# Six more tiles of a second matmul by seven products instead of eight, three tiles ahead of a batch's first

## The chip, the cores and the metric

The kernel runs on one core of one Trainium2 chip. The metric is the time of one execution on the device, in microseconds (us). The engines are TensorE (PE; its weight loads are shown as PEld), VectorE (DVE), ScalarE (ACT), GpSimd (POOL) and SyncE (SP); they run side by side and wait for each other by semaphores. Matmuls write PSUM; VectorE and ScalarE read PSUM and write SBUF; DMA engines move data between SBUF and DRAM, or within SBUF.

## The reference

Two layers follow each other. The first takes x of 8 batches, 3008 positions and 256 channels (float32), transforms it along the positions (a real FFT), mixes the channels of the real and imaginary parts by a complex 256x256 matrix with a bias, shrinks each part towards zero by 0.01, and transforms back:

```
X = np.fft.rfft(x, axis=1)
Yr = Xr @ w_r - Xi @ w_i + b_r
Yi = Xr @ w_i + Xi @ w_r + b_i
Y  = soft_shrink(Yr, 0.01) + 1j * soft_shrink(Yi, 0.01)
y  = np.fft.irfft(Y, n=3008, axis=1)
```

The second takes the 24064 rows of y as tokens:

```
h = y @ w_in                 # 256 -> 2048
g = s * relu(h)**2 + b       # s and b are single numbers
out = g @ w_out              # 2048 -> 256
```

## The kernel before

**Transforms.** 3008 = 94 x 32, so each Fourier transform is two short ones, done as matmuls (helpers `s1_units`, `s23_units`, `s4_units`), with two trips through DRAM for each batch (ud and us, vd and vs). Each unit is one or a few matmuls into a PSUM bank of the pool psf (two banks) and one cast out of it, by VectorE or ScalarE: u (96x512), xf, v (128x512), yt (128x470). The shrinking is a chain of VectorE operations on the tile ring (lines 714 to 716; for the last two pairs of frequencies it is followed by eight copies, line 727). Batch b+1 is transformed while the second layer works on batches before it.

**Second layer.** The tokens are cut into 48 tiles in a fixed order (`_tile_order`): 12 wide ones of batches 0 and 1, then for each of the batches 2 to 7 five main tiles of 512 tokens, and some tail tiles (512 or 384 tokens from the ends of two batches) behind or between them. `mark[b]` is the place of the first tile of batch b, in steps of 1/16 tile: tiles 12, 17, 23, 29, 35 and 41 for batches 2 to 7.

The main loop goes through the tiles, 16 steps each. Step mc of tile ti does three things: planned units of the transforms; the first matmul of 128 hidden rows (`first_mm`, two matmuls of 512 columns into psh, two buffers of two banks); and a sixteenth of the second matmul of the tile before, ti - 1. So a tile's own stretch of time holds its first layer, and its products follow in the next stretch. At every odd step ScalarE takes the ReLU of two banks (line 871, tile rt), and then the square is written to gt in float16, by VectorE (line 884) or ScalarE (line 881). Which engine does a square or a cast is fixed when the program is built: `act_first` compares the estimated loads that `work` has added up. A scheduler then sets the order on each engine.

**Two ways to do the second matmul.** `second_mms` is the plain one: 4 blocks of 128 tokens by 16 blocks of hidden rows, 64 matmuls of 256 columns, and two operations of VectorE (line 945, 128x512) that scale by s, add the bias and write ost. `seven_mms` is a scheme of Strassen and Winograd: hidden rows and tokens are halved, and seven products of sums of quarters replace eight, 112 matmuls of 128 columns. The sums of quarters of the squares (`s_op`, line 980, 128x1024 in float16) are numbered 1 to 4 and made once for each half q of the hidden rows:

```
1: s1  = a21 + a22        3: a21 = a11 - a21
2: a11 = a11 - s1         4: a12 = a12 + a11   (an accumulating DMA from GpSimd's queue, line 973)
```

Sums 1 and 3 of q=0 are put at steps 10 and 11 of the tile's own stretch, the others at steps 2 to 5 of the next. Sums of the right-hand side (T_s) are made once. The products lie in two psa banks that are used in turn: products 1 and 2 share a bank, then product 3, then 4 and 5, then 6 and 7. `leave` takes them out by VectorE: eight operations of line 1012 (ost or zz from psa; seven of 128x256 and one of 128x512) and one of line 1030. Group 0 of `leave` (zz, then ost, then line 1030) empties the bank of products 1 and 2, which product 4 needs at the end of step 6. The seventh product, which reads the result of sum 4, begins at step 13.

`seven(ti)` says which tiles go that way: all full ones from the first tile of batch 7 on save the last two, tiles 4 to 6, and the two tiles ahead of each batch's first tile, as far as they have 480 or 512 tokens: 17 tiles.

**Queues.** GpSimd's queue issues the loads of x (line 234), the accumulating DMAs, and a copy into the tail tile (line 805), in the order that the scheduler gave. SyncE's queue issues the trips through DRAM, 32 KB moves within ring, and the stores.

Of the kernel before, what the change touches and what calls it, by code (L numbers as in the profile page):

```python
# [11 lines left out]
ALU = mybir.AluOpType  # L12
# [84 lines left out]
def kernel(  # L97
# [14 lines left out]
    B, S, D = x.shape  # L112
# [4 lines left out]
    MC = DFF // P  # L117
# [59 lines left out]
    def work(engine, us):  # L177
        load[engine] = max(load[engine], pe["now"]) + us
# [636 lines left out]
    def sub_size(tl):  # L815
        return 4 * tl[3] if tl[0] == "wide" else P
# [13 lines left out]
    def halves(ti):  # L830
        return width(tiles[ti]) in (480, 512)
# [129 lines left out]
    def part(ti, q, i, k):  # L961
        size = 2 * sub_size(tiles[ti])
        return gts[(ti, q)][:, i, k, :, 0:size]

    def s_op(ti, n, q):

        size = 2 * sub_size(tiles[ti])
        if n == 1:
            sums[(ti, q)] = spool.tile([P, 4, 2 * P], F16, name="s1", tag="s1")
        s1 = sums[(ti, q)][:, :, 0:size]  # L970
        a11, a12, a21, a22 = (part(ti, q, i, k) for i in range(2) for k in range(2))
        if n == 4:
            nc.gpsimd.dma_start(out=a12, in_=a11, accum_op=ALU.add)  # L973
            return
        out, a, b, op = {
            1: (s1, a21, a22, ALU.add),
            3: (a21, a11, a21, ALU.subtract),
            2: (a11, a11, s1, ALU.subtract),
        }[n]
        nc.vector.tensor_tensor(out=out, in0=a, in1=b, op=op)  # L980
        work("dve", 0.07 + size / 480.0)

    def seven_mms(ti):
# [76 lines left out]
        for at, n, q in ((2, 2, 0), (2, 1, 1), (2, 4, 0), (3, 3, 1), (4, 2, 1), (5, 4, 1)):  # L1060
            at += alone and at > 3
            slots[at].append(lambda n=n, q=q: s_op(ti, n, q))
# [4 lines left out]
    def seven(ti):  # L1067
        if ti >= len(tiles) - 2 or not halves(ti):
            return False
        firsts = [mark[b] // MC for b in range(2, B)]  # L1070
        return (
            ti >= firsts[-1] or 4 <= ti < 7 or any(m - 2 <= ti < m for m in firsts)
        )

    plan = {}
# [18 lines left out]
    mark = {}  # L1094
# [32 lines left out]
    for ti in range(ti_n + 1):  # L1127
        nxt = [[]] * MC
        if ti:
            nxt = seven_mms(ti - 1) if seven(ti - 1) else second_mms(ti - 1)  # L1130
        for mc in range(MC):
            if ti < ti_n:
                for u in plan.pop(ti * MC + mc, []):
                    u()
                first_mm(ti, mc)
                if mc in (10, 11) and seven(ti):
                    s_op(ti, 1 if mc == 10 else 3, 0)
            for u in nxt[mc]:
                u()
# [31 lines left out]
```

## Time and profile before

| | |
|---|---|
| median of 3 runs | 840.88 us (838.2 to 841.81) |
| the profiled execution | 838.19 us, span 836.4 us |
| granted TensorE clock | 1.00 |
| squares on VectorE, line 884 | 254, of 128x1024 mean 1223 ns |
| squares on ScalarE, line 881 | 130, of 128x1024 mean 1060 ns |
| ReLU on ScalarE, line 871 | 384, of 128x1024 mean 1027 ns |
| sums of quarters, line 980 | 102, 128x1024 some 687 ns |
| products out, line 1012 | 136, 128x256 some 479 ns, 128x512 some 748 ns |
| plain sums out, line 945 | 59, 128x512 some 748 ns |
| sum 4, line 973 | 34, 857 ns on GpSimd, 4.7 us from issue to landing |

How to read it: busy time is the time that an engine has an instruction in it, as a share of the span of 836.4 us; instructions overlap a little at their ends, so the distance from start to start is less than the duration. A matmul's end is modelled, so a busy TensorE is not one at its peak, and here too the distance from start to start counts. The stretches by tile that follow begin at the first psh matmul of a tile.

### The profile page before, as it was taken

Reading aid. Unit: us, or ns where it says so; the run is one execution under the profiler, and the core shown is the slowest. Engines: PE = TensorE matmul, PEld = TensorE weight load, DVE = VectorE, ACT = ScalarE, POOL = GpSimd, SP = SyncE. Lnnn points to the kernel's source line nnn. Section 1 sums busy time; section 2 is a strip of 40 time slices with the busy share of each in tenths; the row PEclk is TensorE's granted clock in tenths of the full one; section 3 lists DMA queues with packets and bytes.
Section 4 is the critical chain, followed back from the end, with each engine's and each line's share of the span. In section 5 each row is a group of like instructions: output and inputs, shape, how many; then the busy total and the mean of one; then the engine's idle time right before and its main releaser. Section 6 shows DMA issues by size and latency. Waiting matters only on the chain.

```text
span 836.4 us, 19090 instructions
## 1 busy us (share of the span) xinstructions
PE 824.2 (99%) x7470; PEld 598.7 (72%) x7470; DVE 698.8 (84%) x1061; ACT 712.2 (85%) x953; POOL 79.8 (10%) x106
## 2 busy tenths in 40 slices
PE   8999999999999999999999999999999999999997
PEld 7857767777677767777677776777767777767765
DVE  5988989978898888877888788787889878889885
ACT  5998988998899989988899888988879888788882
POOL 4550001100011001100010000100001000001000
PEclk9999999999999999999999999999999999999999
DMA  8954578345873378534772258713565133513321
GB/s 201 183 150 103 120 181 213 64 96 132 199 185 65 98 181 198 126 88 116 192 190 65 81 131 206 180 47 97 127 177 138 48 97 90 140 45 76 72 66 61
DMA packets 115516, 105.04 MB, mean 126 GB/s; under 512 B 12646, under 2 KB 100714, under 8 KB 114082
## 3 DMA queue, kind: packets, MB, share of 16 engines
q1 hardware_dynamic: 102498, 80.55, 34.0%
q0 software_dynamic: 12928, 23.27, 17.6%
q8 instruction: 58, 0.95, 0.5%
q14 instruction: 32, 0.26, 0.1%
HBM read 53.52 MB, written 46.66 MB: 120 GB/s over the span
## 4 chain that ended last, share of the span: by engine, by line
PE 81%; DVE 8%; ACT 5%; DMA 3%; issue 2%; POOL 0%; SPq 0%; DVEq 0%; ACTq 0%; POOLq 0%
PE psh L175 33%; PE psa L175 30%; PE psf L175 17%; ACT rt L871 2%; DVE gt L884 2%; DVE gt L980 1%; DMA ring<-ring 1%; DMA x<-in_x_dram 1%; PE psm L175 1%; ACT gt L881 1%; DVE s L980 1%; DVE ost L1012 1%; ACT u L187 1%; DMA vd<-v 0%; DVE zz L1012 0%
## 5 line engine op out<-in xcount | busy, mean ns | idle before, releaser
L871 ACT ACTIVATE rt<-psh 128x1024 f32<-128x1024 f32 (+2 forms) x384 | 387.0, 1009 | 67.4 <-PE psh L175 65.2
L175 PEld LDWEIGHTS <-gt 128*128 128x128 f16 (+1 forms) x3568 | 303.7, 101 | 171.1 <-DVE gt L884 0.5
L175 PE MATMUL psh<-yt,w_in 128*128 128x512 f16 (+1 forms) x1344 | 396.5, 378 | 0.1
L884 DVE TENSOR_TENSOR gt<-rt 128x1024 f16<-128x1024 f32 (+2 forms) x254 | 304.9, 1204 | 88.6 <-ACT rt L871 86.8
L175 PE MATMUL psa<-w_out_t,gt 128*128 128x256 f16 (+3 forms) x2512 | 333.1, 258 | 0.0
L175 PEld LDWEIGHTS <-w_in 128*128 128x128 f16 x1536 | 137.3, 98 | 25.9 <-issue 3.2
L881 ACT ACTIVATE gt<-rt 128x1024 f16<-128x1024 f32 (+2 forms) x130 | 134.8, 1037 | 3.2
L187 ACT CAST u<-psf 96x512 f16<-96x512 f32 x96 | 55.7, 581 | 9.3 <-PE psf L175 8.6
L175 PE MATMUL psa<-T_s,gt 128*128 128x128 f16 (+1 forms) x752 | 63.5, 219 | 0.0
L699 DVE TENSOR_TENSOR ring<-psf,s 128x512 f16<-128x512 f32 x84 | 57.6, 685 | 4.2 <-PE psf L175 3.1
L187 ACT CAST v<-psf 128x512 f16<-128x512 f32 x82 | 47.5, 582 | 14.2 <-PE psf L175 13.3
L973 POOL DMA_DIRECT2D gt<-gt x34 | 31.1, 916 | 262.3 <-PE psh L175 86.3
L234 POOL DMA_DIRECT2D x<-in_x_dram x36 | 19.3, 540 | 386.3 <-PE psf L175 337.7
L175 PEld LDWEIGHTS <-xf 128*128 128x128 f16 x504 | 47.4, 98 | 7.2 <-DVE xf L672 1.7
L175 PE MATMUL psh<-tail,w_in 128*128 128x512 f16 (+1 forms) x192 | 52.1, 352 | 0.0
L175 PE MATMUL psf<-W_g,xf 128*128 128x256 f16 x336 | 50.4, 272 | 0.0
L945 DVE SCALAR_TENSOR_TENSOR ost<-psa,s_bc,bias_bc 128x512 f32<-128x512 f32 (+2 forms) x59 | 43.0, 730 | 4.5 <-PE psa L175 2.3
L187 ACT CAST yt<-psf 128x470 f16<-128x470 f32 (+2 forms) x84 | 43.2, 534 | 3.4 <-PE psf L175 2.2
L187 ACT CAST xf<-psf 128x512 f16<-128x512 f32 x67 | 39.1, 584 | 4.3 <-PE psf L175 4.1
L175 PE MATMUL psf<-x,A_t 94*96 94x512 f16 x102 | 38.9, 382 | 1.7 <-ACT yt L187 0.3
L175 PE MATMUL psf<-C_t,vs 96*128 96x94 f16 (+1 forms) x484 | 37.9, 205 | 0.0
L1012 DVE SCALAR_TENSOR_TENSOR ost<-psa,s_bc,zz 128x256 f32<-128x256 f32 (+1 forms) x64 | 28.8, 479 | 5.4 <-PE psa L175 3.6
(118 smaller groups left out, 758.2 us busy)
## 6 DMA issues: line engine op xcount, KB each, us to landing
out_dram<-ost SPq DMA_DIRECT2D x152, 128.0 KB
ud<-u SPq DMA_DIRECT2D x56, 192.0 KB
us<-ud SPq DMA_DIRECT2D x28, 384.0 KB
vd<-v SPq DMA_DIRECT2D x42, 256.0 KB
vs<-vd SPq DMA_DIRECT2D x14, 768.0 KB
x<-in_x_dram POOLq DMA_DIRECT2D x28, 376.0 KB, 6.5
ring<-ring SPq DMA_DIRECT2D x280, 32.0 KB
gt<-gt POOLq DMA_DIRECT2D x30, 256.0 KB, 4.6
```

The lines of the kernel that those rows point to most:

```text
L175: return nc.tensor.matmul(out, lhs, rhs, **how)
L187: return None, nc.scalar.copy(out=dst, in_=src)
L234: nc.gpsimd.dma_start(out=t[0:N1, i * w : (i + 1) * w], in_=xv[:, c * XCH * D + i * w : c * XCH * D + (i + 1) * w],)
L699: nc.vector.tensor_tensor(out=ring[0][:, i % 4], in0=ps, in1=hold[i // 2][:, i % 2].unsqueeze(1).to_broadcast([P, 2, D]), op=ALU.add,)
L871: nc.scalar.activation(out=rt[:, :, 0:w], in_=ps[:, :, 0:w], func=AF.Relu)
L881: nc.scalar.activation(out=gt, in_=rr, func=AF.Square)
L884: last_square[0] = nc.vector.tensor_tensor(out=gt, in0=rr, in1=rr, op=ALU.mult)
L945: nc.vector.scalar_tensor_tensor(out=ost[0:size, 0:k], in0=ps[0:size, 0:k], scalar=s_bc[0:size], in1=bias_bc[0:size].unsqueeze(1).to_broad ...
L973: nc.gpsimd.dma_start(out=a12, in_=a11, accum_op=ALU.add)
L980: nc.vector.tensor_tensor(out=out, in0=a, in1=b, op=op)
L1012: nc.vector.scalar_tensor_tensor(out=out, in0=of, scalar=s_bc[0:size], in1=other, op0=ALU.mult, op1=ALU.add)
```

## The change

`seven` takes three tiles ahead of a batch's first in place of two. That adds tiles 9, 14, 20, 26, 32 and 38: the fourth tile of batch 1 (in its order of six), the third of batch 2, and the fourth of batches 3, 4, 5 and 6. For these six the fourth sum of q=1 is an addition on VectorE (float16, 128x1024); that of q=0 stays a DMA. Everything else follows from the planner and the scheduler.

```diff
+    def third_last(ti):
+        return any(ti == mark[b] // MC - 3 for b in range(2, B))
+
     def s_op(ti, n, q):
...
-        if n == 4:
+        if n == 4 and not (q == 1 and third_last(ti)):
             nc.gpsimd.dma_start(out=a12, in_=a11, accum_op=ALU.add)
             return
         out, a, b, op = {
             1: (s1, a21, a22, ALU.add),
             3: (a21, a11, a21, ALU.subtract),
             2: (a11, a11, s1, ALU.subtract),
+            4: (a12, a12, a11, ALU.add),
         }[n]
...
         firsts = [mark[b] // MC for b in range(2, B)]
         return (
-            ti >= firsts[-1] or 4 <= ti < 7 or any(m - 2 <= ti < m for m in firsts)
+            ti >= firsts[-1] or 4 <= ti < 7 or any(m - 3 <= ti < m for m in firsts)
         )
```

## The prediction

> **What bounds the kernel now.** I read the busy table first, then the chain that ended last, then busy time by tile, then VectorE in order of time.
>
> ```profile
> PE 824.2 (99%) x7470; PEld 598.7 (72%) x7470; DVE 698.8 (84%) x1061; ACT 712.2 (85%) x953; POOL 79.8 (10%) x106
> PE 81%; DVE 8%; ACT 5%; DMA 3%; issue 2%; POOL 0%; SPq 0%; DVEq 0%; ACTq 0%; POOLq 0%
> ```
>
> TensorE is busy 99% of the span and carries 81% of the chain: a shorter matmul stream shortens the kernel, if nothing else becomes late. VectorE and ScalarE have some 15% left on average. An average hides the stages, so here are five stretches, each exactly the sixteen steps of one tile: the fourth and fifth tile of batch 3, the tail tile behind them, and two tiles at the end of the program with no transform work beside them.
>
> ```profile
> 388.28:405.90 17.62, 17.62 (x127) 12.19 (x125) 15.62 (x25) 15.33 (x22) 0.54 (x1) 1.00 0.56 140
> 405.90:421.33 15.43, 15.43 (x107) 10.32 (x106) 12.46 (x13) 11.80 (x17) 0.93 (x2) 1.00 0.84 211
> 421.33:437.41 16.08, 16.05 (x211) 12.05 (x209) 14.42 (x22) 15.32 (x22) 1.88 (x3) 1.00 0.82 201
> 735.61:747.76 12.15, 12.15 (x84) 7.84 (x81) 9.00 (x12) 9.87 (x11) 0.21 (x1) 1.00 0.15 45
> 747.76:760.92 13.16, 13.16 (x146) 9.38 (x144) 12.88 (x18) 10.68 (x11) 1.70 (x2) 1.00 0.34 71
> ```
>
> Columns: stretch, length, then busy time of PE, weight loads, VectorE, ScalarE, POOL, then granted clock (1.00 throughout), DMA. In the third stretch a seven-product tile leaves its sums: VectorE and ScalarE are busy 14.42 and 15.32 of 16.08. In the second, where the change puts another such tile, they are busy 12.46 and 11.80 of 15.43. That is free time in sum, but the question is when it comes. VectorE in the third stretch, in order of time (start, duration):
>
> ```profile
> 421.53 0.75 DVE L945 SCALAR_TENSOR_TENSOR ost<-psa,s_bc,bias_bc 128x512 f32<-128x512 f32 x1
> 422.20 1.22 DVE L884 TENSOR_TENSOR gt<-rt 128x1024 f16<-128x1024 f32 x1
> 423.34 0.69 DVE L980 TENSOR_TENSOR gt<-gt,s 128x1024 f16<-128x1024 f16 x1
> 423.94 0.69 DVE L980 TENSOR_TENSOR s<-gt 128x1024 f16<-128x1024 f16 x1
> 424.54 1.22 DVE L884 TENSOR_TENSOR gt<-rt 128x1024 f16<-128x1024 f32 x1
> 425.68 0.68 DVE L980 TENSOR_TENSOR gt<-gt 128x1024 f16<-128x1024 f16 x1
> 426.28 0.64 DVE L189 CAST yt<-psf 128x470 f16<-128x470 f32 x1
> 426.84 0.68 DVE L980 TENSOR_TENSOR gt<-gt,s 128x1024 f16<-128x1024 f16 x1
> 427.44 0.48 DVE L1012 SCALAR_TENSOR_TENSOR zz<-psa,s_bc,bias_bc 128x256 f32<-128x256 f32 x1
> 427.95 0.48 DVE L1012 SCALAR_TENSOR_TENSOR ost<-psa,s_bc,zz 128x256 f32<-128x256 f32 x1
> ```
>
> and TensorE at the end of it:
>
> ```profile
> 427.97 0.50 PE L175 MATMUL psa<-T_s,gt 128*128 128x128 f16 x6
> 428.49 0.23 PE L175 MATMUL psa<-T_s,s 128*128 128x128 f16 x1
> ```
>
> VectorE runs without a gap from 421.53 to 428.43. The fourth product (psa<-T_s,s) needs the PSUM bank that the last row frees; six small matmuls take 0.34 us in free running (0.056 each), so TensorE was ready at 428.31 and began at 428.49: a stall of 0.2 us. This hand-over limits such a tile. From the start of L945 to the restart of TensorE it is 6.96 us.
>
> **The change, part by part.** One step is the start-to-start distance in gapless rows, smaller than the printed duration: square 1.14 (422.20 to 423.34), sum 0.60, psf cast 0.56 to 0.60, L945 0.67, L1012 0.40, or 0.51 where it reads its predecessor's output.
>
> *TensorE.* The stretch at 735.61 has 32 matmuls of 512 columns and 48 of 256, the one at 747.76 has 32 of 512 and 112 of 128. A pair of 512 steps 0.43 in the timeline, 6.88 for 32. That leaves 5.27/48 = 0.110 per 256 and 6.28/112 = 0.056 per 128 columns. A tile: 64 x 0.110 = 7.03 before, 112 x 0.056 = 6.28 after, 0.74 us less without rounding. Six tiles: -4.4 us, the whole possible gain, 0.5% of the span. The weight loads, 112 for 64, hide: in the last stretch 144 of them are busy 9.38 of 13.16.
>
> The Trainium skill, "TensorE: Matmul & The Clock Gate", section "Back-to-back issue gap", speaks against this step: in a stream of weight load and matmul pairs it gives about 81 ns per matmul at 128 columns. By that a tile would cost 9.1 us instead of 6.28. The trace disagrees: 0.056.
>
> *VectorE and ScalarE.* Each new tile adds six sums (first two in its own stretch, four in the next), a seventh for the second half of the fourth sum, eight L1012 and one L1030 in place of two L945. The planner answers: 29 squares go from VectorE to ScalarE (254 to 225, 130 to 159), and 15 evacuations of psf the other way (v 82 to 75, yt 84 to 78, u 96 to 94 on ScalarE). In sum VectorE gets 42 x 0.60 + 42 x 0.40 + 6 x 0.67 + 6 x 0.33 - 12 x 0.67 - 29 x 1.14 + 15 x 0.58 = some 15 us, ScalarE 29 x 0.96 - 15 x 0.48 = some 20 us, over six groups of three tiles. The idle time of the three stretches above covers that in sum; its place is what costs.
>
> *The bank in the new tile's stretch* (second row above). In the changed order VectorE has, from L945 to the freeing row, the same ten instructions, except that the yt cast is gone and the new fourth sum stands between the two L1012: -0.56 - 0.51 + 0.40 + 0.60, so 6.89 us instead of 6.96. L945 starts at 406.13 before. In the stretch ahead VectorE runs gapless from 395.3 to 408, and gets two sums (+1.20) and a cast of v (+0.60), loses a square (-1.14), and the sums fill 0.25 of waits in the chain L714 to L716: +0.41, so 406.54, and the bank is free at 413.43. TensorE reaches the fourth product one matmul ahead of the psh pair that starts at 412.85, less 7 x 0.046 for seven shortened steps: 412.48. Stall 0.95. Four of the six new tiles (the fourth of batches 1, 3, 4 and 5) have this order: 4 x (0.95 - 0.74) = +0.8. Bounds: 0.2 (the row above) to 1.5 (VectorE later by another half square). The new sum itself waits for the third sum and for the second product's reading, both over by then; behind it on VectorE stands the row that frees the bank, and TensorE waits for that.
>
> *The third tile of batch 2* (its stretch begins at 282.9, that of its products at 302.4). A cast of v moves to VectorE behind the ring copies, which end at 301.95 before and, by +1.05 of sums and a square taken out behind them, at 302.9 after. TensorE wants that bank at 302.23 and gets it at 303.64: 1.4, while a stall of 0.4 on a v cast by ScalarE behind it goes. Then a second v cast and both squares stay in front: bank free at 312.25, TensorE there at 311.0: 1.25. Together 1.4 - 0.4 + 0.1 + 1.25 - 0.74 = +1.6. Bounds -0.3 and +2.4.
>
> *The fourth tile of batch 6*: no transform of a next batch beside it. VectorE begins 0.05 later, the order is the same; bank free 713.4, TensorE there at 712.8: 0.6 - 0.74 = -0.15.
>
> *The tile behind.* It starts with three L1012 instead of one L945 (+0.53). In the two groups with a 512-wide tail behind (421.3, 622.8) a square stays on VectorE that waits for its ReLU, and ScalarE now squares first: that ReLU moves from 425.08 to 425.6, the bank from 428.4 to 429.3 against TensorE at 428.3: +0.85 each, +1.7; bounds 0 and 1.9. In the other four a square leaves VectorE: -0.2 in the two before a 384-wide tail, 0 and +0.1 in the others, -0.3 in sum.
>
> *POOL and SP.* One accumulating DMA per new tile (0.86 us on POOL, landing in 4.7), behind one load of x and ahead of the next. It waits for the second sum, about as late as that load's own wait before (409.62), and the load is used over a tile later; the result is read by the seventh product, ten steps (9 us) after. If that cover went, the seventh product would wait 1 to 3 us (landings differ by up to 4.6, from 3.2 to 7.8). The stores are as many as before. Nothing for these.
>
> **The sum** (each term holds its share of the -4.4): 0.8 + 1.6 - 0.15 + 1.7 - 0.3 = +3.7; for waits on psf banks behind the moved casts, 0 to 0.3 in a group, I take 0.05, since their next user is a step away: +4.0. Against the profiled execution (838.19, 1.8 more than its span of 836.4) that is 842.2. The median of the runs, 840.88, is 2.7 above it, so I forecast 844.9.
>
> **The rivals.** *The gain survives.* If VectorE is not late at the hand-over, each stall is the 0.2 of the third stretch: 6 x (0.2 - 0.74) = -3.2; with none -4.4, so 836.5 to 837.7. For it: at 421.3 to 437.4 both engines are 90 and 95% busy and TensorE stands 0.2 us. Against it: there L945 starts as soon as its matmuls end, 0.2 us into the stretch, here at 0.64, and TensorE comes 0.5 sooner. It decides below a stall of 0.74.
>
> *The lag does not drain.* ScalarE gets 20 us more; if its ReLUs fall behind in the tiles before and after the batch's first, psh stalls too: another 1 us in each group, +10, 851. Against it: 1.3 us of idle time on VectorE at 429.7 in the tile behind.
>
> *Weight loads bind.* If each small matmul had to wait for its own load, 98 to 101 ns by the rows of the loads, a tile would take 112 x 0.098 = 11.0 for 7.0: 6 x 4 = +24, 865. The stretch at 747.76 is against it: 144 loads and matmuls without a stall. By the 81 ns of the page named above it would be 6 x 2.1 = +12, 853.
>
> *The DMA is late*: 6 x 1 to 3 on top, 851 to 863.
>
> **How the numbers follow.** Stalls as worked out 66%, the gain survives 15%, no drain 13%, DMA late 5%, weight loads 1%. The likeliest case's own bounds are +0.5 and +8: 841 to 849. The range takes in half of the first rival and most of the second: 838.5 to 851. About 0.5% (4.2 us) is what a measurement of this kernel can tell from no change. Slower by more: a little over half of the first case and the last three, 55%. Faster by more: half of the rival, 8%. Between: 37%.
>
> **What would show it.** Waits of PE psa for ost of VectorE, 1.4 us in four places now, become 8 to 10 us in ten or more; the stretch of each new product stays at 15.4 to 15.8 instead of 14.7; a wait of psf<-ring,T_t for a cast of v appears near 302. I am wrong if those stretches are 14.7 to 15.0, or if the added time stands in waits for psh or for DMA.

## The result and the profile after

The changed kernel takes 845.5 us (median of 6 runs, 842.81 to 847.25), the kernel before 839.25 in the same series (837.85 to 841.81). The ratio is 1.0068, 95% interval 1.0051 to 1.0085: slower by more than the 0.5% that can be told from no change. The profiled execution took 844.8 us, its span is 843.0. The forecast was 844.9 us, and "slower by more than that" with a chance of 0.55.

The busy table and the chain of the kernel after:

```profile
PE 822.4 (98%) x7758; PEld 600.1 (71%) x7758; DVE 713.2 (85%) x1131; ACT 732.2 (87%) x967; POOL 84.4 (10%) x112
...
PE 73%; DVE 11%; ACT 6%; DMA 6%; issue 2%; POOL 0%; SPq 0%; DVEq 0%; ACTq 0%; POOLq 0%
```

TensorE has less to do, and its share of the chain falls from 81 to 73%. VectorE, ScalarE and DMA take the rest: TensorE now waits for them in places where it did not.

What TensorE waited for from 195 to 840 us (the sum, how often, the longest), first in the kernel after, then in the kernel before, where a second row (0.3 for a cast of v) is left out:

```profile
PE psa L175 <- DVE ost L1016: 7.6, 10, 1.0
PE psf L175 <- DMA ud<-u: 0.7, 1, 0.7
PE psf L175 <- DMA vs<-vd: 0.5, 1, 0.5
```

```profile
PE psa L175 <- DVE ost L1012: 0.6, 2, 0.3
```

The ten places of the first row are the hand-over of the product bank in all six new tiles and in four of the tiles behind them. Over the whole span the wait for that bank goes from 1.4 us in four places to 8.4 us in twelve; two of them, in tiles 5 and 7, lie ahead of this window and are the same in both kernels (0.23 and 0.58).

Three stretches by tile, the same as before: the tile ahead, the stretch of a new tile's products, the tile behind (length, then busy PE, weight loads, VectorE, ScalarE, POOL, granted clock, DMA):

```profile
390.96:408.58 17.62, 17.62 (x126) 12.19 (x124) 15.70 (x27) 15.50 (x22) 0.54 (x1) 1.00 0.56 143
408.58:424.49 15.91, 14.87 (x154) 10.25 (x153) 14.38 (x20) 14.22 (x19) 1.81 (x3) 1.00 0.86 199
424.49:441.37 16.88, 16.05 (x211) 12.11 (x209) 15.03 (x23) 15.95 (x24) 2.16 (x4) 1.00 0.87 209
```

The middle stretch shows both halves of the story. PE is busy 14.87 of 15.91 us; before it was 15.43 of 15.43. The saving of TensorE is there, and a stall that is larger stands beside it. VectorE and ScalarE have free time left in this stretch (14.38 and 14.22 of 15.91), so it is not their sum that is short. VectorE in order of time shows where the stall comes from:

```profile
409.30 0.74 DVE L945 SCALAR_TENSOR_TENSOR ost<-psa,s_bc,bias_bc 128x512 f32<-128x512 f32 x1
409.96 1.22 DVE L884 TENSOR_TENSOR gt<-rt 128x1024 f16<-128x1024 f32 x1
411.09 0.69 DVE L984 TENSOR_TENSOR gt<-gt,s 128x1024 f16<-128x1024 f16 x1
411.70 0.68 DVE L984 TENSOR_TENSOR s<-gt 128x1024 f16<-128x1024 f16 x1
412.30 1.22 DVE L884 TENSOR_TENSOR gt<-rt 128x1024 f16<-128x1024 f32 x1
413.43 0.69 DVE L984 TENSOR_TENSOR gt<-gt 128x1024 f16<-128x1024 f16 x1
414.23 0.69 DVE L984 TENSOR_TENSOR gt<-gt,s 128x1024 f16<-128x1024 f16 x1
414.83 0.48 DVE L1016 SCALAR_TENSOR_TENSOR zz<-psa,s_bc,bias_bc 128x256 f32<-128x256 f32 x1
415.23 0.68 DVE L984 TENSOR_TENSOR gt<-gt 128x1024 f16<-128x1024 f16 x1
415.83 0.48 DVE L1016 SCALAR_TENSOR_TENSOR ost<-psa,s_bc,zz 128x256 f32<-128x256 f32 x1
```

and TensorE beside the last of these rows:

```profile
414.83 0.50 PE L175 MATMUL psa<-T_s,gt 128*128 128x128 f16 x6
416.37 0.23 PE L175 MATMUL psa<-T_s,s 128*128 128x128 f16 x1 [1.04 <-DVE ost L1016]
```

These are ten instructions of VectorE, from L945 to the row that frees the bank. TensorE was ready at 414.83 + 6 x 0.056 = 415.17 and began at 416.37: a stall of 1.20 us, against 0.74 saved. Three of the four just ahead of that row are sums of the second half of the hidden rows (413.43, 414.23 and 415.23; steps 0.80, 0.60 and 0.60), the other one reads the bank. The sums are needed much later than the bank. That is what the experiments act on. The stretches behind tiles 9, 20, 26 and 32 have this order; behind tiles 14 and 38 two of the three sums stand ahead of the freeing row.

By tile, from tile 9 on, the time is 5.4 us longer (639.0 to 644.4). The other 1.2 us of the spans' difference lie ahead of the first new tile, in the start-up (+0.66) and in tile 5 (+0.51, of which 0.33 is a wait for an accumulating DMA). In all six experiments below that change the new tiles alone, tile 5 has its former length (15.67 us), so I count these as differences between executions.

### The profile page after: what moved, and what is told of

Read it like the earlier page. It is cut to its first block, busy times and chain, and to the rows that moved or that the text cites. A ratio compares the mean times of both kernels' runs of the same rounds, so it can differ in the third digit from the quotient of the medians.

```text
span 843.0 us, 19776 instructions
## 1 busy us (share of the span) xinstructions
PE 822.4 (98%) x7758; PEld 600.1 (71%) x7758; DVE 713.2 (85%) x1131; ACT 732.2 (87%) x967; POOL 84.4 (10%) x112
## 4 chain that ended last, share of the span: by engine, by line
PE 73%; DVE 11%; ACT 6%; DMA 6%; issue 2%; POOL 0%; SPq 0%; DVEq 0%; ACTq 0%; POOLq 0%
PE psh L175 30%; PE psa L175 26%; PE psf L175 16%; ACT rt L871 3%; DVE gt L884 3%; DVE gt L984 2%; DMA vd<-v 2%; DVE ost L1016 1%; DMA x<-in_x_dram 1%; DMA vs<-vd 1%; PE psm L175 1%; DMA gt<-gt 1%; ACT gt L881 1%; DMA ring<-ring 1%; DVE s L984 1%
## 5 line engine op out<-in xcount | busy, mean ns | idle before, releaser
L884 DVE TENSOR_TENSOR gt<-rt 128x1024 f16<-128x1024 f32 (+2 forms) x225 | 270.0, 1204 | 75.0 <-ACT rt L871 73.1
L175 PE MATMUL psa<-w_out_t,gt 128*128 128x256 f16 (+3 forms) x2416 | 300.3, 251 | 0.5 <-DMA gt<-gt 0.3
L881 ACT ACTIVATE gt<-rt 128x1024 f16<-128x1024 f32 (+2 forms) x159 | 165.4, 1040 | 3.9
L175 PEld LDWEIGHTS <-w_in 128*128 128x128 f16 x1536 | 134.9, 98 | 23.7 <-issue 2.2
L175 PE MATMUL psa<-T_s,gt 128*128 128x128 f16 (+1 forms) x1040 | 87.4, 219 | 0.0
L976 POOL DMA_DIRECT2D gt<-gt x40 | 36.4, 910 | 302.7 <-DVE s L984 167.6
L187 ACT CAST v<-psf 128x512 f16<-128x512 f32 x75 | 43.8, 584 | 12.6 <-PE psf L175 11.2
L1016 DVE SCALAR_TENSOR_TENSOR ost<-psa,s_bc,zz 128x256 f32<-128x256 f32 (+1 forms) x88 | 39.5, 480 | 8.9 <-PE psa L175 8.5
L187 ACT CAST yt<-psf 128x470 f16<-128x470 f32 (+2 forms) x78 | 40.3, 532 | 1.8 <-PE psf L175 1.3
L175 PEld LDWEIGHTS <-s 128*128 128x128 f16 (+1 forms) x368 | 26.6, 101 | 20.8 <-DVE ost L1016 7.2
```

Of the source, the lines that this page charges most:

```text
L175: return nc.tensor.matmul(out, lhs, rhs, **how)
L187: return None, nc.scalar.copy(out=dst, in_=src)
L881: nc.scalar.activation(out=gt, in_=rr, func=AF.Square)
L884: last_square[0] = nc.vector.tensor_tensor(out=gt, in0=rr, in1=rr, op=ALU.mult)
L1016: nc.vector.scalar_tensor_tensor(out=out, in0=of, scalar=s_bc[0:size], in1=other, op0=ALU.mult, op1=ALU.add)
```

## The experiments

The theory: a new tile saves TensorE 0.74 us and gets a larger stall at one hand-over, because VectorE's queue puts sums ahead of the row that frees the bank; it is the order, not the amount of VectorE's work. The rivals: VectorE and ScalarE are simply full in the three stretches (then any repair returns as another wait), or the moved squares and casts are what costs.

**Another bank.** Product 4 is written into the free half of product 3's bank in the six new tiles, so that it need not wait for the bank of products 1 and 2.

```diff
+        apart = third_last(ti)
+        firsts = (0, 2, 4, 6) if apart else (0, 2, 3, 5)
...
-        for at, group in ((4 + alone, 0), (6, 1), (11, 2), (15, 3)):
+        last = ((13, 4), (15, 5)) if apart else ((15, 3),)
+        for at, group in ((4 + alone, 0), (6, 1), (11, 2)) + last:
```

> In the six new tiles product 4 goes into the free half of product 3's PSUM bank, products 5 and 6 share the bank that VectorE frees, product 7 has one of its own; VectorE takes product 6 out at step 13 instead of 15. TensorE, VectorE and ScalarE do the same instructions. Theory (the time is lost where product 4 waits for VectorE to free a bank): the six waits of 1.2, 1.2, 1.2, 1.2, 1.0 and 0.5 us go, 6.2 in sum; some of it comes back in the tile behind, where VectorE now stands later against TensorE, so 3.5 to 6 us faster than the changed kernel (845.5), 839.5 to 842. Rival 1 (the small matmuls with their weight loads cost more than counted): no change, 845. Rival 2 (ScalarE's 20 us more of squares delay psh): the waits for the bank go and as much appears before psh, 844 to 846.

Measured: 844.74 us, ratio 1.0066 (1.0042 to 1.009). No gain; expected were 839.5 to 842. The wait is still in all new tiles but 14, only under another name and for another row. Waits over the span, then TensorE and VectorE around one of them:

```profile
PE psa L175 <- DVE zz L1017: 5.7, 5, 1.3
```

```profile
418.57 0.22 PE L175 MATMUL psa<-T_s,s 128*128 128x128 f16 x1
418.62 0.81 PE L175 MATMUL psh<-yt,w_in 128*128 128x512 f16 x3
420.68 0.49 PE L175 MATMUL psa<-T_s,s 128*128 128x128 f16 x6 [1.25 <-DVE zz L1017]
```

```profile
419.62 0.42 DVE L1035 TENSOR_TENSOR zz<-zz,b 128x256 f32<-128x256 f32 x1
420.14 0.48 DVE L1017 SCALAR_TENSOR_TENSOR zz<-psa,s_bc,zz 128x256 f32<-128x256 f32 x1
```

The first matmul of product 4 now runs without a wait (418.57). The second starts at 420.68, right after VectorE's reading of product 3 (420.14 + 0.48), which is the other half of the same bank. So in this program TensorE waits for a bank that VectorE reads, whichever half it writes. (The Trainium skill, "PSUM — Partial Sum Buffer", section "PSUM bank collisions raise a hardware error", says that two engines on one bank and quadrant at once is an error; no run here tried it, but it would be a reason for the wait.) The reading comes behind the same sums, so the late queue is paid again. That says nothing yet between theory and rival.

**The VectorE half of sum 4 later, or nowhere, or twice.** Three kernels act on the new addition itself. In the first its step is 8 instead of 5:

```diff
+            if n == 4 and q == 1 and third_last(ti):
+                at = 8
```

> The VectorE half of the fourth sum in the six new tiles is put at step 8 instead of 5, so behind the operations that free the bank of products 1 and 2; the seventh product needs it at step 13. Theory: the freeing operation comes 0.4 to 0.5 us earlier (it then waits for its predecessor's output, 0.51 instead of 0.40 + 0.60), so 5 waits of about 1.1 become 0.65: 2 to 3 us faster than the changed kernel, 842.5 to 843.5. Rivals (weight loads, ScalarE): no change, 845.

Measured: 846.1 us, 1.0092 (1.0067 to 1.0118). The edit did not do what it says: the scheduler left the addition between the two rows that read the bank, the stretch is 15.91 as before the edit, and two waits for the accumulating DMA come on top (1.9 us). It tests nothing of the order.

In the second both halves of sum 4 are left to the DMA:

```diff
-        if n == 4 and not (q == 1 and third_last(ti)):
+        if n == 4:
```

> Both halves of the fourth sum of the six new tiles by DMA, as in the other 17. Theory: VectorE has one sum less ahead of the freeing operation, 0.5 us per new tile, 2 to 3 us faster than the changed kernel, unless the DMA comes late. Rival (the DMA is late): its second half stands on GpSimd's queue behind a load of x that waits for a buffer, and the seventh product waits for gt of a DMA by 1 to 3 us in five tiles: 3 to 12 us slower than with the theory's gain, 845 to 855.

Measured: 867.15 us, 1.0339 (1.0321 to 1.0357), far over what was expected. TensorE waits for the DMA in five of the six tiles, and GpSimd's queue shows why it is late:

```profile
PE psa L175 <- DMA gt<-gt: 18.8, 5, 4.9
```

```profile
417.55 0.90 POOL L976 DMA_DIRECT2D gt<-gt  x1 [11.12 <-DVE s L984]
418.12 0.87 POOL L234 DMA_DIRECT2D x<-in_x_dram  x1
420.67 0.86 POOL L976 DMA_DIRECT2D gt<-gt  x1 [1.67 <-ACT rt L871]
```

The second accumulating DMA is issued at 420.67, 2.55 us behind a load of x, and the seventh product begins at 432.16 only, 11.5 us after the issue. The longest landing from 415 to 440 us is 11.4, against a median of 4.6 for the 256 KB ones in the kernel after. That the load of x is what slows it is likely by the order, but not shown alone. So without the VectorE half of sum 4 the change would cost some 28 us.

At the bank itself this kernel does what was expected of it. With one sum less ahead, the freeing row starts 6.04 us after L945 instead of 6.53, and TensorE stands 0.71 instead of 1.20 us:

```profile
420.98 0.23 PE L175 MATMUL psa<-T_s,s 128*128 128x128 f16 x1 [0.56 <-DVE ost L1016]
```

That is so in the four stretches in which the new sum stood ahead of the freeing row; in the other two the wait stays as it was (0.31 and 0.81).

In the third both halves are on VectorE:

```diff
-        if n == 4 and not (q == 1 and third_last(ti)):
+        if n == 4 and not third_last(ti):
```

> Both halves of the fourth sum of the six new tiles on VectorE. Theory: one more sum of 0.60 us between the square and the freeing operation, so each of the waits is 0.5 to 0.6 longer: 3 to 3.6 us slower than the changed kernel, 848.5 to 849. Rivals (weight loads, ScalarE): no change, 845; if a late DMA is what costs, faster, 842.

Measured: 843.69 us, 1.0068 (1.0046 to 1.0089), the same ratio as the change. Expected were +3 us. In four of the new stretches the edit did not put one more sum ahead of the freeing row: the first half of sum 4 took the place of the second half, which went behind. It stands between sums 3 and 2, so the freeing row comes 0.2 earlier (6.33 for 6.53 after L945), the stall is 1.0 for 1.2 and the stretch 15.72 for 15.91. Behind tile 38 one sum more did come in front, and there the stretch is longer, 14.98 for 14.81. The tiles behind are up to 0.5 longer, so that from tile 9 on the six additions cost 0.5 us in sum, no more than a load of vs that came later in tile 16 (a wait of 0.94 for 0.48). So VectorE's total has a small price at most beside the place of its rows.

**The order itself.** In the six new tiles the three sums of the second half (3, 2 and 4) are put behind the freeing row on VectorE's queue. No sum is removed. The planner answers by moving four squares from VectorE to ScalarE and four casts of u the other way; in the stretch shown below two squares stay ahead of the freeing row, as before. The main lines:

```diff
-    def s_op(ti, n, q):
+    def s_op(ti, n, q, after=None):
...
+            with tc.issue_after(after):
+                nc.vector.tensor_tensor(out=out, in0=a, in1=b, op=op)
...
-                add(top[:, :, 0:P], hold[1], z[:, 0])
+                hold["free"] = add(top[:, :, 0:P], hold[1], z[:, 0]).ins
...
+        behind = third_last(ti)
+        sums_at = ((2, 2, 0), (2, 1, 1), (2, 4, 0))
+        if not behind:
+            sums_at += ((3, 3, 1), (4, 2, 1), (5, 4, 1))
...
+        if behind:
+            for at, n in ((5, 3), (6, 2), (7, 4)):
+                slots[at].append(lambda n=n: s_op(ti, n, 1, hold["free"]))
```

> In the six new tiles the sums 3, 2 and 4 of the second half are put behind the operation of VectorE that frees the bank of products 1 and 2 (same instructions, another order on VectorE; the planner moves a square and a few casts). From L945 to the freeing row VectorE then has seven instructions instead of ten, 5.2 us instead of 7.1, and TensorE gets there after 5.9. Theory (these ten instructions set the time of a new tile): the waits of psa for ost in the six new stretches, 6.2 us in sum, go; in the tiles behind they stay or grow by up to 0.5 each, so 3.5 to 6 us faster than the changed kernel: 839.5 to 842. Rival 1 (VectorE and ScalarE are short of time over the whole stretch, wherever the wait stands): the wait appears before another product or before psh and the time stays, 844 to 846. Rival 2 (small matmuls cost more): 845.

Measured: 840.36 us (838.97 to 843.28, 12 runs), 1.0019 (1.0006 to 1.0032). VectorE and TensorE in the stretch that had the stall of 1.20:

```profile
411.83 1.22 DVE L884 TENSOR_TENSOR gt<-rt 128x1024 f16<-128x1024 f32 x1
412.97 0.47 DVE L1020 SCALAR_TENSOR_TENSOR zz<-psa,s_bc,bias_bc 128x256 f32<-128x256 f32 x1
413.48 0.48 DVE L1020 SCALAR_TENSOR_TENSOR ost<-psa,s_bc,zz 128x256 f32<-128x256 f32 x1
```

```profile
413.93 0.59 PE L175 MATMUL psh<-yt,w_in 128*128 128x512 f16 x2
414.37 0.50 PE L175 MATMUL psa<-T_s,gt 128*128 128x128 f16 x6
414.70 0.22 PE L175 MATMUL psa<-T_s,s 128*128 128x128 f16 x1
```

L945 starts at 408.83 here, so the freeing row starts 4.65 us after it instead of 6.53, and TensorE comes to product 4 (414.70) and goes on without a wait. The stretches behind tiles 9, 20, 26 and 32 are 14.87 instead of 15.91 (13.83 instead of 14.81 behind tile 38), 0.56 less than in the kernel before. In these stretches the full rival falls, since the same sums fit in another order, and so does the one of the moved squares, since ScalarE has more of them than before. In the four kernels that differ at this place the freeing row starts 6.53, 6.33, 6.04 and 4.65 us after L945, and the stall is 1.20, 1.00, 0.71 and nothing.

By tile, from tile 9 on, 4.1 of the 5.4 us that the change cost come back (644.4 to 640.2). The tiles behind do not: tiles 22 and 34 take 17.03 and 16.93, where the kernel before took 16.08, and the kernel stays 0.2% above it. What is left of the waits for the bank, over the whole span:

```profile
PE psa L175 <- DVE ost L1020: 2.7, 5, 0.8
```

Three of the five (1.9 us) are in tiles behind a new one, the other two are those of tiles 5 and 7 again.

**The opposite: 0.4 us more ahead of the bank.** The first read of the bank is done twice in the six tiles, with the same result.

```diff
-                add(z[:, 0], hold[0], wide(bias_bc))
+                for _ in range(1 + third_last(ti)):
+                    add(z[:, 0], hold[0], wide(bias_bc))
```

> The changed kernel with the first operation of VectorE on the bank of products 1 and 2 (zz from psa, 0.40 us a step) done twice in the six new tiles. Theory: VectorE frees the bank 0.4 us later in each: the waits grow by 0.4 and the kernel by 2 to 2.5 us, 847.5 to 848. Rivals (small matmuls; ScalarE): no change, 845.5.

Measured: 845.06 us, 1.0073 (1.0059 to 1.0087); some 0.4 above the change by the ratios, where +2 to 2.5 was expected. The bank does come 0.5 later after L945 (freeing row at +7.04 instead of +6.53), but the scheduler also changed TensorE's order: a pair of psh matmuls (0.43 us) now runs ahead of product 4. The stall is 1.27 for 1.20, the stretch 15.98 for 15.91. So this experiment is spoilt as a price of a late queue; it only shows that a planner may put other work into a wait.

**The order in all seven-product tiles ahead of batch 7, and in the kernel before.** The same edit, but in all of them, on the changed kernel and on the one before (`alone` is true from batch 7's first tile on):

```diff
-        behind = third_last(ti)
+        behind = not alone
```

> The same order in all tiles of the seven products before batch 7, so also in the tiles behind the new ones. Theory: the waits in the tiles behind (1.0, 1.0, 0.5, 0.5 and smaller) and those in tiles 4 to 6 (0.4, 0.7) go too: 4 us less than with the new tiles alone, 835.5 to 838.5, so a little under the kernel before. Rivals: as with the new tiles alone, 844 to 846.

> The kernel before with that order in its tiles of the seven products ahead of batch 7. Theory: its waits of psa for ost (0.2 to 0.7, 2.3 us in sum) go: 1.5 to 2.5 us faster than before, 836.5 to 837.5. Rivals: no change, 839.

Measured: 843.74 us, 1.005 (1.0034 to 1.0065), and 843.63, 1.0058 (1.004 to 1.0077). Both missed, by 5 to 8 us. The waits over the span, first of the changed kernel with the order, then of the kernel before with it:

```profile
PE psa L175 <- DMA gt<-gt: 5.5, 6, 1.4
...
PE psa L175 <- DVE ost L1020: 1.0, 3, 0.4
```

```profile
PE psa L175 <- DMA gt<-gt: 3.3, 3, 2.2
...
PE psa L175 <- DVE ost L1016: 0.3, 1, 0.3
```

Most of the waits for the bank went, as forecast. In their place stands the accumulating DMA: the second half of sum 4 can start only behind sum 2, which is now later. In the stretches behind tiles 10, 21 and 27 it is issued 9.98, 10.19 and 8.68 us after the stretch began, where the change had 7.02, 7.73 and 6.80, and the seventh product waits for it. The profiled executions of the two were the shortest of their runs (841.61 and 840.34), so the waits of the others are not fully shown by these rows. In the six new tiles that half is on VectorE, so there it had not shown.

**Both edits together.** The second half of sum 4 on VectorE in every seven-product tile ahead of batch 7, with the order; again on both kernels.

```diff
-        if n == 4 and not (q == 1 and third_last(ti)):
+        if n == 4 and not (q == 1 and ti < mark[B - 1] // MC):
```

> z_all with the second half of sum 4 on VectorE in every seven-product tile ahead of batch 7, not in the six new ones alone. In z_all TensorE waited 5.5 us in six places for the accumulating DMA of the second half of sum 4, which starts later there. Theory (the order of VectorE's queue and that DMA are all that costs): those waits go, the waits for ost stay at about 1 us in sum; 843.7 - 5.5 = 838.2 us, bounds 836.5 to 840, so no slower than the kernel before (838.7). Rival (the eleven more sums on VectorE, 0.64 us each in stretches of 16.9 us where VectorE is busy for 15, push its queue back and it returns as waits for ost or psf): half to all of the 7 us comes back, 841.5 to 844 us.

> The kernel before (no new seven-product tiles) with both edits: sums 3, 2 and 4 of the second half behind the ost that frees the first product bank, and sum 4 of the second half on VectorE, in its eleven seven-product tiles ahead of batch 7. Theory: the 3.3 us of waits for the accumulating DMA in before_z and some 3 us of waits for ost before both go: 843.6 - 3.3 = 840.3 by before_z, 838.7 - 1.5 = 837.2 by the kernel before; taken 838.5, bounds 836.5 to 840.5. Rival (VectorE's load): 841 to 844 us. If z_all_v is below this one, the six new tiles have a gain of their own once the order is mended; the 0.74 us of TensorE's work less in each would make it up to 4 us.

Measured: 838.87 us, 1.0005 (0.9995 to 1.0015), and 837.52, 0.999 (0.9977 to 1.0003), against 838.59 of the kernel before. Within the noise all of the 5.7 us that the change cost are back in the first one, and the rival of VectorE's load falls in its strong form: the additions do not return as 3 us of waits. (They are thirteen, not the eleven of the expectations: GpSimd issues 13 accumulating DMAs fewer, eleven of 256 KB and two of 240 KB.) But the kernel without the new tiles has the lower median still; the intervals overlap, and by tile it is 1.3 us shorter from tile 9 on (638.1 for 639.4). The two differ so. The stretch of a new tile's products and the one behind it, with the new tiles:

```profile
406.81:421.68 14.87, 14.86 (x154) 10.25 (x153) 13.71 (x20) 14.49 (x18) 1.81 (x3) 1.00 0.86 200
421.68:438.60 16.92, 16.32 (x211) 12.11 (x209) 14.96 (x24) 16.45 (x24) 1.68 (x3) 1.00 0.80 206
```

and without:

```profile
406.70:422.14 15.44, 15.44 (x107) 10.33 (x106) 12.46 (x13) 11.80 (x17) 0.93 (x2) 1.00 0.84 210
422.14:438.01 15.87, 15.87 (x210) 12.04 (x208) 15.12 (x23) 15.09 (x22) 1.08 (x3) 1.00 0.74 189
```

The new tile gains 0.57 in its own stretch and loses 1.05 in the next, where ScalarE is busy 16.45 of 16.92. ScalarE and then VectorE of the kernel with new tiles in that next stretch:

```profile
423.51 1.03 ACT L871 ACTIVATE rt<-psh 128x1024 f32<-128x1024 f32 x1
424.58 1.06 ACT L881 ACTIVATE gt<-rt 128x1024 f16<-128x1024 f32 x1
425.54 0.53 ACT L187 CAST yt<-psf 128x470 f16<-128x470 f32 x1
425.97 1.03 ACT L871 ACTIVATE rt<-psh 128x1024 f32<-128x1024 f32 x1
```

```profile
425.52 0.68 DVE L985 TENSOR_TENSOR s<-gt 128x1024 f16<-128x1024 f16 x1
427.03 1.22 DVE L884 TENSOR_TENSOR gt<-rt 128x1024 f16<-128x1024 f32 x1 [0.83 <-ACT rt L871]
```

A square that the planner moved to ScalarE (424.58) stands between two ReLUs. VectorE's next square waits 0.83 for the second ReLU, behind that square is the freeing row, and TensorE waits 0.52 for the bank and soon 0.40 for a cast. Here the rival of the full engines has its case: in two of the six groups ScalarE has hardly any room for the squares. That is read from these rows; no run puts that square back on VectorE.

**Two new tiles only.** The stretch behind cost 1.04 at tiles 22 and 34, but only 0.34 and 0.22 at 28 and 40. So only tiles 26 and 38 are kept; they were chosen from the run just told.

```diff
-            ti >= firsts[-1] or 4 <= ti < 7 or any(m - 3 <= ti < m for m in firsts)
+            ti >= firsts[-1] or 4 <= ti < 7 or any(m - 2 <= ti < m for m in firsts) or ti in (26, 38)
```

> before_z_v with two of the six new tiles, 26 and 38. In z_all_v against before_z_v the new tile's stretch was 0.56 us shorter at all of 21, 27, 33 and 39 (0.51 at 39), but the stretch behind it 1.04 longer at 22 and 34 (16.92 against 15.88) and only 0.34 and 0.22 longer at 28 and 40; so tiles 26 and 38 should each leave a gain, 0.22 and 0.29 us. Theory (what a new tile is worth hangs on the stretch behind it, whose load differs from tile to tile): stretches 27 and 28 together 29.4, 39 and 40 together 28.2, 0.5 us less than before_z_v (837.5), so 837.0 us, 836 to 838; against the kernel before (838.6) a ratio of 0.998. Rival (the planner gives other engines the squares of other tiles when two tiles change, and a wait returns elsewhere): 838 to 840 us.

Measured: 838.14 us (836.37 to 839.88, 12 runs) against 838.86, ratio 0.9984 (0.9972 to 0.9996). It is the one kernel whose interval lies below 1, by less than the 0.5% named in the prediction. The stretches came out as expected, 27 and 28 together 29.44 and 39 and 40 together 28.26. That the two tiles add something to the order alone (0.9984 against 0.999, intervals that overlap) is shown by the stretches, 0.5 us, and not by the times.

## Why the prediction was right, and where its terms were off

The time (844.9 for 845.5), the sign and the mechanism were right: the waits of the product bank for VectorE went from 1.4 us in four places to 8.4 in twelve over the span, where 8 to 10 in ten or more were named. Four of the new stretches are 15.91, a little over the 15.4 to 15.8 that were named. That the total came so near is luck, as the last point of this list shows. Terms, one by one:

- **TensorE, -4.4.** Held. In the mended order the new stretches are 0.56 shorter, and 0.50 behind tile 38. The missing 0.18 of 0.74 is no wait for VectorE: in z_new's new stretch the one stall left is a wait of 0.18 for a ReLU, at step 12. Weight loads did not bind: with 112 small matmuls the stretch was 14.87, which also settles the prediction's sentence on 81 ns, by whose estimate it would be 15.43 + 2.1.
- **The bank in the new stretch, +0.8 for four tiles.** Measured 4 x 0.48 = +1.9. The start of L945 was good: 406.54 was forecast, 2.69 us earlier than the 409.23 of this execution's time, where it is 409.30. TensorE's own time (412.48, here 415.17) was exact. The step that failed is "so 6.89 us": it is 7.07 to TensorE's restart. I took 0.60 for every sum. Sum 2 overwrites the quarter that sum 3, just ahead of it, reads, and the step between them is 0.80 (413.43 to 414.23); in the rows of 421.53 to 427.95 the yt cast stood between them and hid it. Elsewhere the kernel before has that step, 0.79 to 0.80 us, seven times, so it could have been read there. Taking an instruction out of a queue gave back 0.36, not its 0.56.
- **The third tile of batch 2, +1.6.** Measured +0.3 (+0.89 in its own stretch, -0.59 in the next). The v cast behind the ring copies is there, as the two rows below show, but both parts were too large: the stall is 0.9 and not 1.4, since one of the two sums ahead of the copies fell into an idle gap of 0.54 us (before the square that starts at 295.96 in the kernel before), so that the copies end 0.4 later and not 0.95; and the bank's is 0.48 and not 1.25. VectorE, then TensorE:

```profile
302.37 1.86 DVE L727 COPY ring<-ring 64x256 f16<-64x256 f16 x8
304.26 0.69 DVE L189 CAST v<-psf 128x512 f16<-128x512 f32 x1
```

```profile
305.00 0.38 PE L175 MATMUL psf<-ring,T_t 128*128 128x256 f16 x2 [0.72 <-DMA ud<-u]
```

  The profile names a DMA for that wait; in seven of the experiments the same wait has the label "DVE v L189", and by the times it is the cast.
- **The fourth tile of batch 6, -0.15.** Measured +0.48: a stall of 0.97 for 0.6. Two sums of the second half stand in front here, and the first square waits 0.52 for its ReLU.
- **The tile behind, +1.7 and -0.3.** The two with a 512-wide tail are +0.80 each (forecast 0.85), by the mechanism named. TensorE there:

```profile
432.59 0.22 PE L175 MATMUL psa<-T_s,s 128*128 128x128 f16 x1 [0.83 <-DVE ost L1016]
```

  The other four were forecast to gain 0.3 and lost 1.07. Of that 0.5 is in tile 16, where a load of vs came later (a stall of 0.64 for 0.18), for which the prediction had no term.
- **POOL, SP and the DMA, nothing.** Right for this change: no wait for the accumulating DMA from tile 9 on. How thin the cover is was not foreseen, as the experiments with the DMA show.
- **The sum.** +5.4 from tile 9 on, for +4.0. The undersized bank and tile-behind terms (+1.1, +0.6, +1.4 and -0.1) and the oversized one of batch 2 (-1.3) partly offset each other, and the 0.3 for psf banks did not appear apart from the wait at 305. What closes the rest is the base: +4.0 was added to a median of 840.88 from three runs, and in the series of the result the kernel before has 839.25. From that base the forecast would have been 843.3. The medians differ by 6.25 us where 4.0 was forecast, so the agreement of the total to 0.6 us is luck; the sign and the place of the waits are not.

Of the rivals, "the gain survives" needed a stall below 0.74, and it was 1.20. It does survive once the sums stand behind the freeing row, but in most groups only inside the new stretch. "The lag does not drain" is wrong for the change as a whole, and right in the small: the stretch behind tiles 21 and 33 is full. "The DMA is late" was kept off by the VectorE half of sum 4, as the kernel without it shows.

## What to carry to other kernels

When less matmul work is bought with more vector work, ask for each hand-over which instructions stand in the queue ahead of the one that frees the buffer, and whether those are needed before it: here three additions that put a freeing row back by 1.9 us cost more than the whole saving, with free time on every engine of the stretch. Repair the order first, then look for what now starts later; the sums moved back made a DMA late by 2 to 3 us that nobody had waited for. And even when a change is repaired, judge it against the old kernel with the same repair: here the repair alone (0.999) came out no worse than the repair with the change (1.0005), and neither differs from the kernel before by more than its interval.

## What the runs showed of the hardware that was not expected

- The step of an addition of 128x1024 in float16 behind another is 0.60 us where the two have no operand in common, and 0.71 to 0.80 where the second overwrites what the first reads (in the kernel before 0.71 to 0.73 from sum 1 to sum 3, 0.79 to 0.80 from sum 3 to sum 2). That the overwriting is the reason is read from these pairs; no run tried it alone. An unrelated cast between sums 3 and 2 costs 0.36 net, not 0.56.
- An accumulating DMA of 256 KB takes 4.6 us in the median from issue to landing, and at most 8.2 in the kernel after. In the kernel that leaves both halves of sum 4 to the DMA it takes up to 12.3; the one of 11.4 has a load of x of 376 KB ahead of it in the same queue.
- In three stretches of that kernel TensorE waits 4.0 to 4.9 us for the DMA. There the granted TensorE clock is 0.94 to 0.95, where the stretches shown above have 1.00, and the same matmuls are busy some 16.05 us instead of 14.87. So a long wait cost more here than its own length; no run varied the wait alone.
